# Reordering the first loads, copies and sines of a gated FFT/GEGLU backward kernel

## The chip, the cores and the metric

The kernel runs on one core of a Trainium2 chip. The metric is device time in microseconds (us) for one execution of the whole program. Engines are named as in the profile: PE (TensorE), DVE (VectorE), ACT (ScalarE), POOL (GpSimd) and SP (SyncE, which here only issues DMAs).

## The reference

The program computes a forward result and the gradients for all inputs but B_x. There are two branches over the same x of 2048 rows by 576 columns: a 2-D real FFT, multiplied with a complex weight and transformed back, and a gated GELU feed-forward of inner width 4608. A sigmoid gate per row mixes them.

```
x = A_x
g = sigmoid((x * gate_w).sum(-1, keepdims=True))
a = irfft2(rfft2(x) * (w_r + 1j * w_i))
b = (gelu(x @ w_gate) * (x @ w_up)) @ w_down
out = g * a + (1 - g) * b
outputs: out, and the gradients of x, w_r, w_i, w_gate, w_up, w_down, gate_w for a given grad_out (dO)
```

## The kernel before

**Stages.** The first part runs over 18 groups g of 256 columns of the inner width, and in each over four steps m of four row tiles (128 rows each). A step computes z = dO w_down^T and xy = x [w_gate | w_up], squeezes them through the GELU and its derivative, and stores A, dHu and dHg to DRAM scratch. Matmuls for the gradients of the weights of the group before, and units of the FFT branch, are put between. A last part multiplies the stored tiles with the weights for b and the gradient of x; it takes the last 428 us or so and is pure PE work.

**Order.** The order of the work is written out by hand: each engine runs its instructions in the order of the program text, and the framework only adds the semaphores. A DMA that is issued from SP may first wait for an older DMA whose semaphore it takes over.

**Head.** [...]dO, x and w_down are transposed by PE. `titems` (L367) returns three closures for four row tiles: column chunks 0 and 1, chunks 2 and 3, chunk 4. Each transposes into one PSUM tile (L378, L381, L384) and copies it out (L385) by the engine that is passed: `VC` is a DVE copy, `AC` an ACT copy. The PSUM tiles come from `pgtile` and `phtile`, two buffers each, so a third closure on the same kind of tile waits for the first one's copy. Ahead of the loop stand: 30 dummy matmuls (L896), six small ones that lay gate_w on partitions (L901) and their casts to gwT (L905, L907), sine tables for the columns (`build_D`: y on POOL or DVE at L130 and L131, the angles on DVE at L136 and L138, the sines on ACT at L141 and L142), the transposes of dO tiles 0 to 3 into dOT, and those of the first 256 rows of w_down (wdn) into wdT.

**First step, g = 0 and m = 0.** `H_mm` issues z's matmuls over chunks 0 to 3 (L413), then `opening` (L918), then z's last chunk (L418) and the first part of xy (L422). `opening` transposes x tiles 0 to 3, makes the second and third group of sines, `parity` (L107 to L110), the masked tail tables (`tails`, L148 to L152), the row angles of tiles 0 to 3 (`build_R`, L165 and L172), and the gate of these four tiles (`gate`, L390: 20 matmuls at L394, a sigmoid at L396, two small ACT instructions). Then follow the transposes of dO tiles 4 to 7 (`do1`), the rest of xy (L429), the transposes of x tiles 4 to 7 (`x1`), the evacuation of xy by ACT (`H_act`, L448 to L451), row angles of tiles 4 to 7 (`build_R`, L169 to L172), small column constants (`columns_B`, L187 on), the gate of the next four tiles, the first third of the transposes of dO tiles 8 to 11 (`do2`), and the first half of the elementwise work (`H_ew1`, L456 to L460, DVE). Its second half (`H_ew2`, L476 to L497) runs within the next step, as `held`. The same pattern with fewer transposes holds for m = 1 and m = 2.

Of the kernel before, what the change touches and what calls it, by code (L numbers as in the profile page):

```python
# [9 lines left out]
ACT = mybir.ActivationFunctionType  # L10
ALU = mybir.AluOpType
BF16 = mybir.dt.bfloat16
# [27 lines left out]
LO, HI = slice(0, 64), slice(64, 128)  # L40
# [4 lines left out]
def eo(c):  # L45

    return slice(256 * (c % 2) + c // 2, 256 * (c % 2) + 256, 2)
# [41 lines left out]
def iotas_R(nc, tb, res, unit):  # L89
    G, V = nc.gpsimd, nc.vector  # L90
    kw = dict(allow_small_or_imprecise_dtypes=True)
    tb.qcol_i = res.tile([P, 1], I32, name="qcol_i")
    G.iota(tb.qcol_i[:], pattern=[[0, 1]], base=0, channel_multiplier=1)
    kk = tb.kk = unit([2, P], F32, name="kk")
    tb.krow = kk[:, 0, :].rearrange("p (g k c) -> p g k c", k=2, c=2)
    for v in range(2):
        G.iota(tb.krow[:, :, v, :], pattern=[[1 - 2 * v, 32], [0, 2]], base=64 * v, channel_multiplier=0, **kw)
    G.memset(tb.krow[:, 0, 1, :], 32.0)
    tb.kadd = kk[:, 1, :].rearrange("p (k c) -> p k c", c=2)
    G.iota(tb.kadd, pattern=[[0, 64], [S // 4, 2]], base=S // 4, channel_multiplier=0, **kw)  # L100
    tb.scol = res.tile([P, T], F32, name="scol")
    G.iota(tb.scol[:], pattern=[[1, T]], base=0, channel_multiplier=16, **kw)
    par_i = res.tile([P, 1], I32, name="par_i")
    tb.par = res.tile([P, 2], F32, name="par_f")

    def parity():
        V.tensor_single_scalar(par_i[:], tb.qcol_i[:], 1, op=ALU.bitwise_and)  # L107
        V.tensor_copy(tb.par[:, 1:2], par_i[:])
        V.tensor_scalar(tb.par[:, 0:1], tb.par[:, 1:2], -1.0, 1.0, op0=ALU.mult, op1=ALU.add)
        V.tensor_scalar(tb.kadd[:, 0, 1:2], tb.par[:, 1:2], float(S // 2), float(S // 4), op0=ALU.mult, op1=ALU.add)  # L110
    return parity
# [7 lines left out]
def build_D(nc, tb, unit, c0, n):  # L119

    V = nc.vector
    step = 2.0 * math.pi / D
    TS = (nc.gpsimd if c0 else V).tensor_scalar
    X = unit([n, HF], F32, name="XD")
    y = unit([n, HF], F32, name="yD")
    for c in range(n):
        TS(y[:, c, :], tb.lrow[:], tb.dn[:, c0 + c:c0 + c + 1], MAGIC, op0=ALU.mult, op1=ALU.add)  # L130
    TS(y[:], y[:], -MAGIC, -float(D), op0=ALU.add, op1=ALU.mult)  # L131
    o = unit([n, 2, HF], name="Dt")

    def angles():
        for c in range(n):
            V.scalar_tensor_tensor(X[:, c, :], tb.lrow[:], tb.dcol[:, c0 + c:c0 + c + 1], y[:, c, :],  # L136
                                   op0=ALU.mult, op1=ALU.add)
        V.scalar_tensor_tensor(y[:], X[:], -1.0, X[:], op0=ALU.mult, op1=ALU.max)  # L138

    def sines():  # L140
        nc.scalar.activation(o[:, :, 0, :], y[:], ACT.Sin, bias=tb.halfpi[:], scale=-step)  # L141
        nc.scalar.activation(o[:, :, 1, :], X[:], ACT.Sin, scale=-step * EPS_SCALE)  # L142
        if c0 < 4:
            tb.Dt += [o[:, c] for c in range(n)]

    def tails():
        tl = unit([2, 2, 2, HF], name="Dt")
        nc.gpsimd.memset(tl[HI, 0], 0.0)  # L148
        nc.gpsimd.memset(tl[LO, 1], 0.0)
        for k, r in enumerate((LO, HI)):  # L150
            for par in range(2):
                V.tensor_scalar(tl[r, k, par], o[r, 0], tb.par[r, par:par + 1], None, op0=ALU.mult)  # L152
        tb.Dt += [tl[:, k, par] for k in range(2) for par in range(2)]
    return angles, sines, tails
# [101 lines left out]
def kernel(  # L256
# [4 lines left out]
    nc = tc.nc  # L261
    LD = nc.sync
# [6 lines left out]
    unit = Unit(ctx.enter_context(tc.tile_pool(name="unit", bufs=NUNIT, side="right")), "unit")  # L269
# [27 lines left out]
    wts = {}  # L297
# [26 lines left out]
    def load_x(t0):  # L324
        LD.dma_start(xn[:, t0:t0 + 4, :], x_v[:, t0:t0 + 4, :])

    def load_do(t0):
        LD.dma_start(dB[:, t0:t0 + 4, :], do_v[:, t0:t0 + 4, :])

    ident = res.tile([P, P], BF16, name="ident")  # L330
    make_identity(nc, ident[:])
    gwr = unit([D], name="gwr")
    nc.scalar.dma_start(gwr[0:1, :], gate_w.rearrange("(o d) -> o d", o=1))
    load_do(0)
    wdn = unit([2, D], name="wdn")
    LD.dma_start(wdn[:], B_w_down[0:FG, :].rearrange("(c p) d -> p c d", p=P))
    load_x(0)
    load_w(0, 0, nc.scalar)
    for k in range(1, 4):
# [2 lines left out]
    tb = iotas(nc, res, unit)  # L342
# [27 lines left out]
    def titems(src, dst, t0, ps, copies, n=4):  # L370

        def item(k, cs):
            def f():
                tp_ = ps[k](BF16).rearrange("p (j t m) -> p j t m", j=2, t=4)
                for j, c in enumerate(cs):
                    for tt in range(n):
                        if c < 4:
                            nc.tensor.transpose(tp_[:, j, tt, :], src[:, t0 + tt, eo(c)], ident[:])  # L378
                        elif n < 4:
                            for r in (LO, HI):  # L380
                                nc.tensor.transpose(tp_[r, 0, tt, :], src[:, t0 + tt, 512:D], ident[:])  # L381
                        else:
                            c0 = (t0 + tt) * D + (512, D - P)[tt % 2]
                            nc.tensor.transpose(tp_[:, 0, tt, :], src[:].rearrange("p t d -> p (t d)")[:, c0:c0 + P], ident[:])  # L384
                copies[k](dst[:, cs[0]:cs[0] + len(cs), t0:t0 + n, :], tp_[:, 0:len(cs), 0:n, :])  # L385
            return f
        return [item(k, cs) for k, cs in enumerate(((0, 1), (2, 3), (4,)))]

    def gate(k):
        lps = pgtile()  # L390
# [510 lines left out]
        nc.tensor.matmul(gps[r, c:c + 1], lhsT=w, rhs=one[:], start=True, stop=True)  # L901
    D0 = build_D(nc, tb, unit, 0, 2)
    D0[0]()
    D0[1]()
    AC(gwT[:, 0:4], gps[:, 0:4])  # L905
    for c, r in ((4, LO), (5, HI)):
        AC(gwT[r, c:c + 1], gps[r, c:c + 1])  # L907
    D2 = build_D(nc, tb, unit, 2, 2)
    D2[0]()
    D4 = build_D(nc, tb, unit, 4, 1)  # L910
    parity = iotas_R(nc, tb, res, unit)
    for f in titems(dB, dOT, 0, (pgtile, pgtile, phtile), (VC, AC, VC)):
        f()
    for f in titems(wdn, wts[0][1][:].rearrange("p k (c m) -> p k c m", c=2), 0, (phtile, pgtile, phtile), (AC, VC, VC), n=2):
        f()
    makeB = build_B(nc, tb, unit, res)

    def opening():  # L918
        for f in titems(xn, xT, 0, (pgtile, pgtile, pgtile), (VC, AC, VC)):
            f()  # L920
        D2[1]()
        D4[0]()
        D4[1]()
        parity()
        D4[2]()
        build_R(nc, tb, unit, 0)
        gate(0)

    fg = zipped(*fwd_units(xT, scr_x, None)) + zipped(*fwd_units(dOT, scr_g, gs32))
# [62 lines left out]
    for g in range(NG):  # L992
# [3 lines left out]
        for m in range(NPR):  # L996
# [15 lines left out]
            if g == 0:  # L1012
# [28 lines left out]
                for part in range(2):  # L1041
                    H_act(1, xy, tiles, part)
                if m == 0:
                    build_R(nc, tb, unit, 4)
                    columns_B(nc, tb, res)
                elif m == 1:
                    next(makeB)
# [312 lines left out]
```

## Time and profile before

| | |
|---|---|
| median of 3 runs | 1395.96 us (1395.55 to 1396.18) |
| the profiled execution | 1396.09 us, span 1394.3 us |
| PE clock granted | 1.00 |
| z of m=0, 1, 2, 3 starts at | 8.60, 21.76, 30.73, 39.58 us |
| z of the second group starts at | 45.64 us |

The span is what the engines' instructions cover; the device time has a little more at both ends. A timeline row reads: start in us, duration in us, engine, line, operation, output and inputs, shapes, number of merged instructions, and in brackets how long the engine was idle before and what ended it. Durations of merged rows overlap a little with the row behind them, so the distance from start to start is the better measure of a rate.

Where the DMAs stand in the head:

| load, in order of SP's queue | issued at us | landed at us |
|---|---|---|
| dO tiles 0 to 3, 576 KB | 0.75 | no record; first used at 5.12 |
| wdn, 288 KB | 1.20 | 5.8 |
| x tiles 0 to 3, 576 KB | 1.67 | 7.9 |
| w_gate of group 0, 256 KB | 2.18 | no record |
| w_up of group 0, 256 KB | 4.93 | no record |
| dO and x tiles 4 to 7 | 6.11, 7.79 | no record; first used at 13.88 and 17.81 |
| dO and x tiles 8 to 11 | 8.17, 8.64 | 15.2, 16.5 |
| dO and x tiles 12 to 15 | 9.12, 9.62 | 18.0, 19.6 |

### The profile page before, as it was taken

Reading aid. Unit: us, or ns where it says so; the run is one execution under the profiler, and the core shown is the slowest. Engines: PE = TensorE matmul, PEld = TensorE weight load, DVE = VectorE, ACT = ScalarE, POOL = GpSimd, SP = SyncE. Lnnn points to the kernel's source line nnn. Section 1 sums busy time; section 2 is a strip of 40 time slices with the busy share of each in tenths; the row PEclk is TensorE's granted clock in tenths of the full one; section 3 lists DMA queues with packets and bytes.
Section 4 is the critical chain, followed back from the end, with each engine's and each line's share of the span. In section 5 each row is a group of like instructions: output and inputs, shape, how many; then the busy total and the mean of one; then the engine's idle time right before and its main releaser. Section 6 shows DMA issues by size and latency. Waiting matters only on the chain.

```text
span 1394.3 us, 25930 instructions
## 1 busy us (share of the span) xinstructions
PE 1372.9 (98%) x10186; PEld 914.3 (66%) x10272; DVE 740.2 (53%) x1406; ACT 710.8 (51%) x1311; POOL 245.6 (18%) x486
## 2 busy tenths in 40 slices
PE   8999999999999999999999999999999999999999
PEld 6556566566566556556566566556777777777777
DVE  7975656555889777885656666560001742211101
ACT  7877767777787878767767777661000000000000
POOL 3001011123345634412111101110000100000000
PEclk9999999999999999999999999999999999999999
DMA  6433445355466656555556465749999998777873
GB/s 216 126 86 110 132 108 132 92 146 157 114 165 157 154 143 164 144 142 135 148 141 170 127 164 154 176 110 279 195 193 200 230 192 169 162 156 166 154 153 90
DMA packets 510646, 214.49 MB, mean 154 GB/s; under 512 B 312538, under 2 KB 503708, under 8 KB 510524
## 3 DMA queue, kind: packets, MB, share of 16 engines
q1 hardware_dynamic: 493402, 187.44, 57.9%
q0 software_dynamic: 14912, 24.24, 6.2%
q8 instruction: 80, 1.31, 0.4%
q10 hardware_dynamic: 2210, 1.15, 0.4%
q14 instruction: 42, 0.34, 0.1%
HBM read 41.05 MB, written 93.84 MB: 97 GB/s over the span
## 4 chain that ended last, share of the span: by engine, by line
PE 90%; ACT 2%; issue 1%; DMA 0%; SPq 0%; DVE 0%; ACTq 0%
PE acc L1210 30%; PE wps L559 16%; PE xy L429 15%; PE wps L541 9%; PE z L413 8%; PE wps L573 2%; PE xy L422 2%; PE pf L602 2%; PE z L418 1%; PE pf L619 1%; PE pf L873 1%; PE pf L800 1%; PE pf L711 1%; PE pf L875 1%; ACT ZT L850 0%
## 5 line engine op out<-in xcount | busy, mean ns | idle before, releaser
L1210 PEld LDWEIGHTS <-pin 128*128 128x128 bf16 x3456 | 338.0, 98 | 85.8 <-issue 0.5
L559 PE MATMUL wps<-dH,xn 128*128 128x512 bf16 x1135 | 269.9, 379 | 1.3 <-DVE dwd L510 0.5
L429 PE MATMUL xy<-wgu,xT 128*128 128x512 bf16 x1083 | 258.2, 379 | 8.3 <-issue 7.0
L429 PEld LDWEIGHTS <-xT 128*128 128x128 bf16 x1152 | 106.5, 98 | 133.0 <-issue 24.8
L559 PEld LDWEIGHTS <-xn 128*128 128x128 bf16 x1152 | 111.5, 98 | 118.6 <-issue 1.3
L1227 ACT COPY bo<-acc 128x288 f32<-128x288 f32 x32 | 12.8, 399 | 305.0 <-PE acc L1210 305.0
L541 PE MATMUL wps<-dB,A 128*128 128x288 bf16 x1152 | 154.2, 286 | 0.7 <-DVE dB L990 0.6
L566 POOL DMA_DIRECT2D out_dram<-dw x134 | 73.0, 548 | 430.4 <-ACT dw L510 389.3
L1210 PE MATMUL acc<-wgT,pin 128*128 128x288 bf16 x1152 | 143.8, 286 | 0.0
L1210 PE MATMUL acc<-wuT,pin 128*128 128x288 bf16 x1152 | 143.6, 286 | 0.0
L1210 PE MATMUL acc<-wd_all,pin 128*128 128x288 bf16 x1152 | 142.6, 286 | 0.0
L413 PE MATMUL z<-wdT,dOT 128*128 128x256 bf16 x1152 | 137.5, 272 | 1.0 <-ACT wdT L385 0.5
L541 PEld LDWEIGHTS <-A 128*128 128x128 bf16 x1152 | 112.1, 98 | 34.3 <-issue 1.3
L441 ACT ACTIVATE da<-z,omg 128x256 bf16<-128x256 f32 x288 | 112.3, 473 | 32.9 <-PE z L418 32.8
L413 PEld LDWEIGHTS <-dOT 128*128 128x128 bf16 x1152 | 112.5, 98 | 23.1 <-issue 2.2
L450 ACT CAST xb<-xy 128x512 bf16<-128x512 f32 x144 | 85.3, 593 | 48.0 <-PE xy L429 47.6
L1282 DVE SCALAR_TENSOR_TENSOR f32t<-gwf,dlog,b16t 128x576 f32<-128x576 f32 x16 | 13.1, 817 | 172.2 <-DMA b16t<-dxa_scr 172.2
L448 ACT ACTIVATE q<-xy 128x512 bf16<-128x512 f32 x144 | 87.9, 614 | 7.0 <-PE xy L429 4.7
L451 ACT CAST hu<-xy 128x512 bf16<-128x512 f32 x144 | 87.5, 608 | 0.0
L487 DVE TENSOR_TENSOR xb<-xb,sg 128x1024 bf16<-128x1024 bf16 x48 | 33.1, 691 | 96.6 <-ACT sg L479 96.5
L510 ACT CAST dw<-wps 128x512 bf16<-128x512 f32 x72 | 42.3, 590 | 54.5 <-PE wps L559 52.3
L456 DVE TENSOR_SCALAR s<-q 128x1024 bf16<-128x1024 bf16 x72 | 30.6, 425 | 69.9 <-ACT q L448 69.7
(220 smaller groups left out, 1636.7 us busy)
## 6 DMA issues: line engine op xcount, KB each, us to landing
scr<-dH SPq DMA_DIRECT2D x144, 256.0 KB, 3.4
scr<-A SPq DMA_DIRECT2D x72, 256.0 KB, 2.7
out_dram<-dw POOLq DMA_DIRECT2D x134, 64.0 KB, 2.5
wd_all<-in_B_w_down_dram SPq DMA_DIRECT2D x3, 1728.0 KB, 9.9
out_dram<-dwd POOLq DMA_DIRECT2D x34, 144.0 KB, 2.9
scr_p<-Vt SPq DMA_DIRECT2D x32, 145.0 KB, 2.9
wgu<-in_B_w_gate_dram SPq DMA_DIRECT2D x18, 256.0 KB, 4.1
wgu<-in_B_w_up_dram SPq DMA_DIRECT2D x18, 256.0 KB, 3.4
```

What stands on the lines that cost most here:

```text
L413: nc.tensor.matmul(zo(t), lhsT=dOT[:, ci, t, :], rhs=wdT[:, ci, :], start=(t % 4 < 2 and ci == 0), stop=False)
L429: nc.tensor.matmul(xy[k][:, t % 2, :], lhsT=xT[:, ci, t, :], rhs=wgu[:, ci, :], start=False, stop=(ci == 3))
L441: nc.scalar.activation(da[:, t, :], z[:, t % 2, t // 2, :], ACT.Copy, scale=omg32[:, 4 * m + t:4 * m + t + 1])
L448: nc.scalar.activation(q[:, h, :], xy[:, :, 0:FG], ACT.Square)
L450: nc.scalar.copy(xb[:, h, :], xy[:, :, 0:FG])
L451: nc.scalar.copy(hu[:, h, :], xy[:, :, FG:2 * FG])
L487: V.tensor_tensor(xb[:], xb[:], s[:], op=ALU.mult)
L510: wcopy[0](out, in_)
L541: nc.tensor.matmul(wps[:, :288], lhsT=tl(0, t)[:, fch * P:(fch + 1) * P], rhs=dB[:, t, h * 288:(h + 1) * 288], start=(t == 0), stop=(t == ...
L559: nc.tensor.matmul(wps[:].rearrange("p a b -> p (a b)"), lhsT=xn[:, t, c * P:(c + 1) * P], rhs=kt[t // 4][1][:, t % 4].rearrange("p k f -> ...
L566: wst[0].dma_start(ov[:, c, fsl], dw[:, k, :])
L1210: nc.tensor.matmul(acc[:, :288], lhsT=src[:, r, :], rhs=w_of(r)[:, h * 288:(h + 1) * 288], start=(first and r == 0), stop=(last and r == F ...
```

## The change

Six edits, none of which changes what is computed:

- wdn is loaded ahead of dO, and dO tiles 0 to 3 come in two DMAs of two tiles.
- The casts to gwT go from ACT to DVE.
- wdn is transposed ahead of dO, its copies by DVE, ACT, DVE (before: ACT, DVE, DVE).
- dO tiles 0 to 3 are transposed by pairs of tiles, four chunks into one PSUM tile (`pair`), copied by DVE and ACT; their chunk 4 stays with `titems`. The first sines, `D0[1]`, come behind that.
- In `opening` the sines of D2 and D4 come ahead of the transposes and copies of x, and a one-column sigmoid, whose result nobody uses, behind them. The angles of D4 move ahead of the loop.
- `parity`, the tail tables and the row angles of tiles 0 to 3 move from `opening` to the end of step m = 0, ahead of the row angles of tiles 4 to 7.

```diff
-    def load_do(t0):
-        LD.dma_start(dB[:, t0:t0 + 4, :], do_v[:, t0:t0 + 4, :])
+    def load_do(t0, n=4):
+        LD.dma_start(dB[:, t0:t0 + n, :], do_v[:, t0:t0 + n, :])
...
-    load_do(0)
     wdn = unit([2, D], name="wdn")
     LD.dma_start(wdn[:], B_w_down[0:FG, :].rearrange("(c p) d -> p c d", p=P))
+    load_do(0, 2)
+    load_do(2, 2)
     load_x(0)
...
+    def pair(src, dst, t0, ps, cp):
+
+        tp_ = ps(BF16).rearrange("p (c t m) -> p c t m", c=4, t=2)
+        for c in range(4):
+            for tt in range(2):
+                nc.tensor.transpose(tp_[:, c, tt, :], src[:, t0 + tt, eo(c)], ident[:])
+        cp(dst[:, 0:4, t0:t0 + 2, :], tp_)
...
     D0 = build_D(nc, tb, unit, 0, 2)
     D0[0]()
+    VC(gwT[:, 0:4], gps[:, 0:4])
+    for c, r in ((4, LO), (5, HI)):
+        VC(gwT[r, c:c + 1], gps[r, c:c + 1])
+    for f in titems(wdn, wts[0][1][:].rearrange("p k (c m) -> p k c m", c=2), 0, (phtile, pgtile, phtile), (VC, AC, VC), n=2):
+        f()
+    pair(dB, dOT, 0, pgtile, VC)
+    pair(dB, dOT, 2, pgtile, AC)
+    titems(dB, dOT, 0, (None, None, phtile), (None, None, VC))[2]()
     D0[1]()
-    AC(gwT[:, 0:4], gps[:, 0:4])
-    for c, r in ((4, LO), (5, HI)):
-        AC(gwT[r, c:c + 1], gps[r, c:c + 1])
     D2 = build_D(nc, tb, unit, 2, 2)
     D2[0]()
     D4 = build_D(nc, tb, unit, 4, 1)
+    D4[0]()
     parity = iotas_R(nc, tb, res, unit)
-    for f in titems(dB, dOT, 0, (pgtile, pgtile, phtile), (VC, AC, VC)):
-        f()
-    for f in titems(wdn, wts[0][1][:].rearrange("p k (c m) -> p k c m", c=2), 0, (phtile, pgtile, phtile), (AC, VC, VC), n=2):
-        f()
...
     def opening():
+        D2[1]()
+        D4[1]()
+        nc.scalar.activation(tb.warm[:], tb.halfpi[:], ACT.Sigmoid)
         for f in titems(xn, xT, 0, (pgtile, pgtile, pgtile), (VC, AC, VC)):
             f()
-        D2[1]()
-        D4[0]()
-        D4[1]()
-        parity()
-        D4[2]()
-        build_R(nc, tb, unit, 0)
         gate(0)
...
                 if m == 0:
+                    parity()
+                    D4[2]()
+                    build_R(nc, tb, unit, 0)
                     build_R(nc, tb, unit, 4)
                     columns_B(nc, tb, res)
```

## The prediction

> **What bounds the kernel now.** I read the shares of busy time first. TensorE (PE) fills the span, so a change at the head pays only if it moves the time at which PE works on, and keeps it moved until the stages behind it.
>
> ```profile
> PE 1372.9 (98%) x10186; PEld 914.3 (66%) x10272; DVE 740.2 (53%) x1406; ACT 710.8 (51%) x1311; POOL 245.6 (18%) x486
> ```
>
> Next the timeline of the head, engine by engine. ScalarE (ACT) first: after its copy of x it runs four sines and loads a table before the sigmoid of the gate.
>
> ```profile
> 8.60 1.91 PE L413 MATMUL z<-wdT,dOT 128*128 128x256 bf16 x16 [0.52 <-ACT wdT L385]
> 11.44 1.01 ACT L385 COPY xT<-pf 128x1024 bf16<-128x1024 bf16 x1 [2.89 <-PE pf L378]
> 12.35 0.54 ACT L141 ACTIVATE Dt<-yD,halfpi 128x290 bf16<-128x290 f32 x1
> 12.50 0.69 PE L394 MATMUL pf<-gwT,xT 128*128 128x1 bf16 x20 [0.38 <-ACT xT L385]
> 13.95 1.28 ACT L396 ACT_TABLE_LOAD   x1
> 15.47 0.61 PE L378 MATMUL pf<-ident,dB 128*128 128x128 bf16 x8 [0.97 <-ACT g_bf L396]
> ```
>
> The bracket is the idle time before the instruction and what ended it: z waits for the last wdT copy, the gate for ACT's copy of x, and the second transpose of the next dO for the sigmoid. Then VectorE (DVE), from the end of step m=0:
>
> ```profile
> 19.82 1.02 DVE L385 COPY xT<-pf 128x1024 bf16<-128x1024 bf16 x2 [0.62 <-PE pf L378]
> 20.76 0.22 DVE L169 TENSOR_SCALAR k<-kk 128x128 int32<-128x128 f32 x1
> 23.28 0.42 DVE L456 TENSOR_SCALAR s<-q 128x1024 bf16<-128x1024 bf16 x1
> 25.34 0.42 DVE L385 COPY dOT<-pf 128x512 bf16<-128x512 bf16 x1
> 28.03 1.02 DVE L385 COPY xT<-pf 128x1024 bf16<-128x1024 bf16 x2 [2.27 <-PE pf L378]
> 36.21 0.42 DVE L385 COPY dOT<-pf 128x512 bf16<-128x512 bf16 x1
> 36.68 0.61 PE L378 MATMUL pf<-ident,xn 128*128 128x128 bf16 x8 [0.17 <-DVE dOT L385]
> 67.70 3.08 PE L541 MATMUL wps<-dB,A 128*128 128x288 bf16 x20 [0.61 <-DVE dB L990]
> ```
>
> Last, busy time by stretch (PE, PEld, DVE, ACT, POOL, clock, DMA share, GB/s):
>
> ```profile
> 8.60:13.10 4.50, 3.78 (x56) 3.35 (x55) 1.60 (x4) 1.66 (x3) 0.00 (x0) 1.00 1.01 355
> 28.00:44.00 16.00, 15.62 (x163) 10.27 (x163) 14.72 (x27) 14.32 (x31) 1.61 (x6) 1.00 0.28 83
> 44.00:60.00 16.00, 15.33 (x96) 8.28 (x95) 14.87 (x27) 11.95 (x22) 0.00 (x0) 1.00 0.33 100
> ```
>
> The reader is to see two regimes. Up to about 20 us DVE has room (1.60 of 4.50 us). From 28.0 to 68 us it works almost without a break (14.7 and 14.9 of 16 us), and PE stands behind it at 36.68 (dOT copy) and at 67.70 (scaled dB). The ACT wait on L457 at 44.68, behind which PE waits for hu at 48.70, belongs to the same chain. **So what counts is not when z starts but when DVE gets to its 28.03 copies.**
>
> **What the Trainium skill says.** "ScalarE: Activation LUTs", section "What ACT_TABLE_LOAD costs", gives 1283 ns for the load and about 1380 ns of drain. The trace agrees on the load (1.28 us) and shows no drain: L396 starts at 15.24, 1.29 us after the load. I take 1.28. "TensorE: Matmul & The Clock Gate", section "What's actually happening", has PE at half clock until some 3.4 us of activity, and again after an idle window of that length. The trace agrees for the start: 16 weight loads of dB take 1.62 us from 5.12, 100 ns each, while 8 of wdn from 7.04 take 0.49, some 60 each; nothing here shows a return to the low clock, since no wait of the head is longer than 1.4 us. The same page ("Architectural detail") calls ACT and DVE strict first-in first-out; the timelines agree, and it is why each moved instruction delays all that is queued behind it.
>
> **Part 1: loads.** wdn (288 KB) goes ahead of dO, and dO's 576 KB come in two halves. The bytes up to the end of dO are the same, and wdn now lands last at 5.83, so the second half lands there, the first half with wdn at about 4.9 (dO, 576 KB, is there at 5.12 today). One more DMA is one more SP issue (0.42 us) ahead of xn, the weights and the later tiles. SP's issues also wait for older transfers (u at 4.93 waits 2.0 us for dB), so g, u and dB(1) may leave up to 2 us later. Bounds: 0 to +0.7 us of arrival. xn landed at 7.9 and is used at 10.24, later tiles have more room: I take nothing.
>
> **Part 2: first copies.** gwT's three casts go from ACT (6.14 to 6.50) to DVE, where they fit between the first angles (end 4.85) and the first wdT copy: nothing. D2's angles (4.77 to 5.90) go behind the dO copies, D4's (0.71) behind those. PE: 12 transposes of wdn from 5.12 at 100 ns end at 6.3, pair 0 is through at 7.0, pair 1 at about 7.5, the last chunk at 7.7. Copies start 0.38 us after the eighth weight load, as at 6.20 today: pair 0 on DVE 7.40 to 8.09, chunk 4 to 8.46; pair 1 on ACT 7.8 to 8.8. z starts on pair 0 at 8.12 and its second half at 8.97 finds pair 1 ready: **z starts 0.48 us earlier**, and so do the transposes of x (9.76).
>
> **Part 3: ACT ahead of x.** Behind pair 1 ACT now has, in start-to-start times of today's rows: copy 0.91, D0 0.76 (5.38 to 6.14), D2 0.77, D4 0.65 (13.30 to 13.95), table 1.28, small sigmoid 0.11. D2's angles are done by 9.5, D4's by 10.2, in time. 7.8 + 4.48 = 12.3: only then the copy of x, which PE would have had ready at 10.96. It ends at 13.36, and **the gate starts at 13.42 instead of 12.50, 0.92 later**. In return the sigmoid follows at once. From gate to L429 PE needs 0.62 (gate), 0.12, 0.64, 0.47 and 0.39 = 2.24 us (rows 12.50 to 14.35 without the wait, then 15.47 to 15.86), where it took 3.36. L429 starts at 15.66 instead of 15.86: a gain g of 0.2 us. DVE's copies at 19.82 move by the same.
>
> **Part 4: masks and row angles.** Parity, four masks and the first row angles leave 13.12 to 16.52 on DVE (3.40 less 0.26 of waiting = 3.1 us), which costs PE nothing there. They go between 20.76's row angles and the copies before, on a DVE with 2.55 us of small work and H_ew1 ahead. The two POOL memsets (0.58, 0.57) move with them; POOL is idle from 7.8 to 23.5: nothing. The dOT copy of 25.34 moves by 3.1 - 0.2 = 2.9 and ends at 28.68. The x transposes of m=1 need its PSUM buffer, as 36.68 shows for m=2. They start at 27.17 now, start at 28.73 then: **+1.56 us**; the 2.27 us idle before 28.03 absorbs the rest. Behind this DVE is full up to 68 us and PE follows it, so the whole delay is kept; after that PE sets the pace, and nothing in the page is tied to absolute time.
>
> **Sum.** +1.56 against the own span of 1394.3, whose run took 1396.09, beside a median of 1395.96 over runs 0.63 apart: 1395.96 + 1.5 = **1397.5 us**. In general: shift = 1.76 - g, and g = 13.62 - (start of the gate).
>
> **Rivals.** (A, 58 in 100) as above, own range 1396.3 to 1398.7, from g of -0.7 to 1.2. (B, 22) The pause of PE ahead of the gate, from about 11.4 to 13.4 with 0.5 before it, brings the low clock back. For: the page's idle window. Against: matmuls lie in most windows of 3.4 us. Up to 3.4 us of work at half speed cost 1.7, so g = -1.5 and the shift 3.3: 1399.2. (C, 20, not slower) The ACT queue isn't in the way: pair 1 is copied early, the sines overlap z, and x is copied when PE has it, gate at about 11.9. Place: ACT between pair 1 and x; price: 1.5 us of the 4.48; it decides from a gate start of 11.86, where 1.76 - g is zero. For: ACT idles 2.89 us there today. Against: seven rows with measured durations. With z at 7.5 the gate starts at 11.4: -0.45, so 1395.5. That wdn lands no sooner for being issued first would be a rival on Part 2 alone: z at 8.6, ACT at 8.3, half a microsecond worse, inside A.
>
> **Chances and range.** About 0.2%, 2.8 us, is what a measurement of this kernel can tell from no change. A lies within it but for its upper tail (8 of 58, for delays that later stages add); B lies above; C is within it, except that another order of loads and buffers may shorten waits later (PE idles 21 us in all): 7 of its 20. Faster 0.07, same 0.63, slower 0.30. Range for 8 in 10: from 1394.4 (most of C) to 1400.2 (B with 1 us of drift).
>
> **What would show it.** z near 8.1; gate near 13.4 behind an ACT copy at 12.3 that follows a table load; no wait for g_bf; DVE without its 2.27 us pause before the x copies of m=1, and PE waiting there 1.5 us for dOT; the 67.70 matmul at about 69.2. A gate before 11.9, or DVE idle again in m=1, would prove the forecast wrong.

## The result, and the profile after

| | before | after |
|---|---|---|
| median of 6 runs each | 1395.78 us (1395.53 to 1396.18) | 1400.36 us (1397.79 to 1401.99) |
| ratio, 95% interval | | 1.0032 [1.0019, 1.0044] |
| profiled execution, span | 1394.3 us | 1399.6 us |
| granted PE clock in it | 1.000 | 0.997 |

The change makes the kernel 4.6 us slower, and wide: before, six runs lie within 0.65 us, after within 4.2. The forecast was 1397.5 us with a range up to 1400.2; the median lies just above the range. The first sign of the reason is in the table: the clock isn't full. Of the six executions after, the two at a clock of 1.000 took 1397.79 and 1399.03 us, the four below it 1400.20 to 1401.99.

The timeline of PE in the profiled execution after (start, duration, what ran, and in brackets the idle time before it with what ended it). L403 is the gate (L394 before), L438 the rest of xy (L429), L385 the last chunk of the x transposes (L384), L550 the first gradient of the weights (L541).

```profile
7.46 0.62 PE L395 MATMUL pf<-ident,dB 128*128 128x128 bf16 x8 [0.29 <-DMA dB<-in_grad_out_dram]
8.14 2.09 PE L422 MATMUL z<-wdT,dOT 128*128 128x256 bf16 x16
13.79 0.64 PE L403 MATMUL pf<-gwT,xT 128*128 128x1 bf16 x18 [1.24 <-ACT xT L386]
17.43 0.63 PE L438 MATMUL xy<-wgu,xT 128*128 128x512 bf16 x1
18.28 2.48 PE L438 MATMUL xy<-wgu,xT 128*128 128x512 bf16 x6 [0.22 <-issue]
32.40 0.38 PE L385 MATMUL pf<-ident,xn 128*128 128x128 bf16 x4 [1.24 <-DVE dOT L386]
41.59 0.61 PE L379 MATMUL pf<-ident,xn 128*128 128x128 bf16 x8 [0.51 <-DVE dOT L386]
72.61 3.08 PE L550 MATMUL wps<-dB,A 128*128 128x288 bf16 x20 [0.61 <-DVE dB L998]
```

z starts at 8.14, as forecast (8.12). The gate starts at 13.79 (forecast 13.42, before 12.50). Then comes what the forecast gave a chance of 22 in 100: six matmuls of L438 take 2.48 us from 18.28, some 410 ns each, where the kernel before ran seven in 1.89 (270 each, with their overlap):

```profile
15.91 1.89 PE L429 MATMUL xy<-wgu,xT 128*128 128x512 bf16 x7
```

The z of m=1, at 24.72, is 2.96 us late; z of m=2 (35.29) is 4.56 late, z of m=3 (44.49) 4.91, L550 at 72.61 4.91, and the first matmul of the last part, at 971.48, 4.86. So all but 0.4 us of what is lost is lost by 45 us and then kept; the 0.4 are lost behind the last matmul (see e9 and e10).

ACT's timeline after shows why the gate is late:

```profile
8.12 1.01 ACT L396 COPY dOT<-pf 128x1024 bf16<-128x1024 bf16 x1 [1.33 <-PE pf L395]
9.03 0.54 ACT L141 ACTIVATE Dt<-yD,halfpi 128x290 bf16<-128x290 f32 x1
11.33 1.28 ACT L932 ACT_TABLE_LOAD   x1
12.73 0.99 ACT L386 COPY xT<-pf 128x1024 bf16<-128x1024 bf16 x1
14.46 0.17 ACT L405 ACTIVATE g_bf<-pf 128x4 bf16<-128x4 f32 x1 [0.73 <-PE pf L403]
```

From the dO copy to the copy of x lie 4.61 us without a gap (forecast 4.48), and the dO copy itself comes 0.32 us after its forecast 7.8, since PE had to wait for the second half of dO (0.29 us at 7.46). The sigmoid then follows without a table load, as meant.

Two stretches of the profile after (stretch, its length, busy time of PE, PEld, DVE, ACT and POOL with their instructions, granted PE clock, DMA share, GB/s):

```profile
10.30:13.70 3.40, 1.39 (x21) 1.06 (x18) 1.26 (x3) 3.37 (x7) 0.00 (x0) 0.97 1.02 407
13.75:20.20 6.45, 6.20 (x48) 3.73 (x50) 1.38 (x2) 2.14 (x7) 0.00 (x0) 0.50 1.02 342
```

While ACT works through its queue, PE is busy for 1.39 of 3.40 us. Right behind that the clock is 0.50 for 6.8 us, with PE then busy 6.20 of 6.45. In the kernel before, the emptiest stretch of that length holds 2.05 us of PE work, and the clock in its profile stays at 1.00:

```profile
12.10:15.50 3.40, 2.05 (x38) 1.44 (x37) 2.95 (x13) 3.25 (x8) 0.00 (x0) 1.00 1.02 384
```

DVE's timeline after, end of step m=0:

```profile
29.43 0.43 DVE L465 TENSOR_SCALAR s<-q 128x1024 bf16<-128x1024 bf16 x1
30.38 0.69 DVE L466 TENSOR_TENSOR s<-xb,s 128x1024 bf16<-128x1024 bf16 x1 [0.53 <-DVE s L465]
31.93 0.42 DVE L386 COPY dOT<-pf 128x512 bf16<-128x512 bf16 x1
32.26 1.01 DVE L386 COPY xT<-pf 128x1024 bf16<-128x1024 bf16 x2
35.84 1.12 DVE L501 TENSOR_SCALAR xb<-s 128x1024 bf16<-128x1024 bf16 x1
```

The 2.27 us that DVE idled before its x copies of m=1 are gone (31.93 to 32.26, no bracket): the moved masks fill them, and PE waits 1.24 us for the dOT copy at 32.40. Two things there were in no forecast: L466 starts 0.95 us after L465, with 0.53 idle, and L501 takes 1.12 us. In the kernel before, the counterpart of L466 comes 0.52 us behind that of L465 (which starts at 23.28), and that of L501 takes 0.43:

```profile
23.80 0.69 DVE L457 TENSOR_TENSOR s<-xb,s 128x1024 bf16<-128x1024 bf16 x1
31.62 0.43 DVE L492 TENSOR_SCALAR xb<-s 128x1024 bf16<-128x1024 bf16 x1
```

### The profile page after: what moved, and what is told of

It reads as the page before. It is cut to its first block, busy times and chain, and to the rows that moved or that the text cites. A ratio compares the mean times of both kernels' runs of the same rounds, so it can differ in the third digit from the quotient of the medians.

```text
span 1399.6 us, 25934 instructions
## 1 busy us (share of the span) xinstructions
PE 1375.9 (98%) x10186; PEld 915.0 (65%) x10272; DVE 741.5 (53%) x1409; ACT 710.8 (51%) x1309; POOL 247.5 (18%) x486
## 3 DMA queue, kind: packets, MB, share of 16 engines
q8 instruction: 80, 1.31, 0.4%
q10 hardware_dynamic: 2210, 1.15, 0.3%
## 4 chain that ended last, share of the span: by engine, by line
PE 92%; ACT 3%; DVE 3%; issue 1%; DMA 1%; SPq 0%; DVEq 0%; ACTq 0%
PE acc L1221 30%; PE wps L568 16%; PE xy L438 16%; PE wps L550 10%; PE z L422 8%; PE wps L582 2%; PE xy L431 2%; PE pf L611 2%; PE z L427 2%; PE pf L628 1%; PE pf L882 1%; PE pf L809 1%; PE pf L720 1%; PE pf L884 1%; PE pf L856 0%
## 5 line engine op out<-in xcount | busy, mean ns | idle before, releaser
L438 PE MATMUL xy<-wgu,xT 128*128 128x512 bf16 x1083 | 259.5, 380 | 8.5 <-issue 7.2
L438 PEld LDWEIGHTS <-xT 128*128 128x128 bf16 x1152 | 107.0, 98 | 133.9 <-issue 26.5
L550 PE MATMUL wps<-dB,A 128*128 128x288 bf16 x1152 | 154.2, 286 | 0.7 <-DVE dB L998 0.6
L550 PEld LDWEIGHTS <-A 128*128 128x128 bf16 x1152 | 112.1, 98 | 34.3 <-issue 1.4
L465 DVE TENSOR_SCALAR s<-q 128x1024 bf16<-128x1024 bf16 x72 | 30.6, 425 | 69.9 <-ACT q L457 69.5
```

The lines of the kernel that those rows point to most:

```text
L438: nc.tensor.matmul(xy[k][:, t % 2, :], lhsT=xT[:, ci, t, :], rhs=wgu[:, ci, :], start=False, stop=(ci == 3))
L550: nc.tensor.matmul(wps[:, :288], lhsT=tl(0, t)[:, fch * P:(fch + 1) * P], rhs=dB[:, t, h * 288:(h + 1) * 288], start=(t == 0), stop=(t == ...
```

## The experiments

Each kernel is the changed one ("after") or the one before, with the edit shown. "Gate", "L438", "z" are starts less those of the kernel before (12.50; 15.91 with L438's counterpart L429; 21.76, 30.73, 39.58 for z of m=1, 2, 3; 966.62 for the first matmul of the last part), each from one profiled execution (where the gate's row is split, its longer part counts); the span is against 1394.3. In the expectations theory 1 is the account by a late gate, masks on DVE and the half clock; the other theories and rivals are explained there.

| kernel | median us | before, same chip | ratio [95%] | gate | L438 | z m=1 | z m=2 | z m=3 | last part | span |
|---|---|---|---|---|---|---|---|---|---|---|
| after (profile above) | 1400.36 | 1395.78 | 1.0032 [1.0019, 1.0044] | +1.29 | +1.52 | +2.96 | +4.56 | +4.91 | +4.86 | +5.3 |
| e0, after again | 1399.53 | 1396.01 | 1.0021 [1.0014, 1.0028] | -0.09 | -1.00 | +0.37 | +1.97 | +2.31 | +2.24 | +4.2 |
| e1, filler | 1398.44 | 1395.87 | 1.0020 [1.0013, 1.0027] | +1.24 | +0.03 | +0.02 | +1.63 | +1.98 | +1.93 | +3.5 |
| e2, masks back | 1397.66 | 1395.87 | 1.0011 [1.0005, 1.0018] | +0.68 | -0.54 | -0.54 | -0.54 | -0.54 | -0.62 | -0.2 |
| e3, masks only | 1396.54 | 1395.87 | 1.0006 [0.9998, 1.0015] | +0.08 | +0.08 | +0.08 | +1.24 | +0.92 | +0.86 | +0.9 |
| e4, sines back | 1397.73 | 1395.87 | 1.0013 [1.0007, 1.0020] | -0.53 | -0.72 | -0.72 | +0.86 | +1.21 | +1.15 | +1.6 |
| e5, columns first | 1399.40 | 1396.01 | 1.0025 [1.0016, 1.0033] | +0.61 | -0.29 | -0.29 | +1.93 | +1.60 | +1.53 | +2.0 |
| e6, sines only | 1394.97 | 1396.01 | 0.9991 [0.9985, 0.9998] | -0.25 | -1.37 | -1.10 | -1.10 | -1.11 | -1.14 | -1.1 |
| e7, combined | 1394.78 | 1396.01 | 0.9991 [0.9985, 0.9998] | -0.86 | -1.99 | -1.71 | -1.71 | -1.71 | -1.80 | -1.4 |
| e8, POOL later | 1398.46 | 1396.07 | 1.0016 [1.0006, 1.0025] | +0.46 | -0.76 | -0.76 | +0.84 | +1.19 | +1.14 | +3.5 |
| e9, loads only | 1397.85 | 1396.07 | 1.0013 [1.0007, 1.0020] | +0.70 | +0.96 | +2.37 | +2.37 | +2.37 | +2.37 | +2.8 |
| e10, combined, old loads | 1396.13 | 1396.07 | 0.9997 [0.9989, 1.0005] | -0.42 | -1.54 | -1.27 | -1.27 | -1.27 | -1.32 | -1.3 |
| e11, POOL held | 1398.46 | 1396.10 | 1.0014 [1.0007, 1.0020] | +0.33 | -0.89 | -0.89 | +0.10 | -0.23 | -0.05 | +0.4 |

The row of e1 shows how to read it: the gate is 1.24 late, the wait for the sigmoid that is gone makes that good by L438, the masks cost 1.96 between z of m=1 and of m=3, and it is kept until the last part. From there to the span of 3.5 another 1.6 us are lost, of which more below.

### e0: the change once more

No edit.

> The changed kernel as it is, beside the others on this chip. Theory 1 (moved DVE work costs 1.9 us at the start of group 1, PE's clock halved for one or two windows costs 1.5 us each): executions with a mean clock of 1.000 at about 1397.8 us, those at 0.999 at about 1399.3, at 0.997 to 0.998 at 1400.5 to 1402; median near 1400. Rival: the spread is that of the loads, and goes across the clocks.

19 executions, 1397.53 to 1402.24 us. Sorted by their granted clock they fall apart: eight at 1.000 have the median 1397.66 (1397.53 to 1398.04), seven at 0.999 have 1399.93, four at 0.997 or 0.998 have 1401.4. At full clock the kernel takes the forecast's 1397.5 within 0.2 us; the groups below full clock, 11 of 19 executions, lie 2.3 and 3.7 us higher. (The median of all 19, 1399.53, is inside the forecast's range, 2.0 above its middle.) In the profiled execution of e0 (clock 0.999) the clock is at half from 14.27 us for 3.41 us (columns as above),

```profile
14.27:17.68 3.41, 3.19 (x15) 1.67 (x14) 1.38 (x2) 1.02 (x3) 0.00 (x0) 0.50 1.01 409
```

and in the one above from 13.5 us for 6.83, twice as long. So there can be one stretch of 3.4 us at half clock, or two.

### e1: filler matmuls in PE's pause

```diff
+        fill = phtile()
+        for _ in range(30):
+            nc.tensor.matmul(fill[:, :P], lhsT=ident[:], rhs=ident[:], start=True, stop=True)
         gate(0)
```

> The changed kernel plus 30 dummy matmuls of the identity between the transposes of x tiles 0 to 3 and the gate (they fill PE's pause of about 2 us there; nothing else moves). Theory 1 (two costs: DVE work moved into a stretch where DVE is full, shift 1.76 - g; and, in most executions, PE's clock halved from about 13.5 us because of the pause): the clock stays 1.00, g = 13.62 - 13.8 = -0.2, so +1.9 us, about 1397.7 us, and all executions within 0.7 us of each other. Theory 2 (all of the loss is the moved DVE work; the halved clock is hidden behind DVE): 1400.4 us as for the change. Theory 3 (the loads in their new order are late, PE waits for data): 1400.4 us.

PE's timeline with the filler:

```profile
11.64 1.84 PE L937 MATMUL fx<-ident 128*128 128x128 bf16 x30
13.74 0.60 PE L403 MATMUL pf<-gwT,xT 128*128 128x1 bf16 x18 [0.23 <-ACT xT L386]
15.94 1.89 PE L438 MATMUL xy<-wgu,xT 128*128 128x512 bf16 x7
29.47 0.38 PE L385 MATMUL pf<-ident,xn 128*128 128x128 bf16 x4 [1.25 <-DVE dOT L386]
```

The gate is as late as in the kernel after (13.74), but L438 runs at full speed and starts at 15.94 rather than 17.43, and 20 of 21 executions have a clock of 1.000. **That the pause of PE brings the low clock back is thereby shown**: work of no use in the pause takes it away, with loads, ACT's queue and masks unchanged. The shift of z of m=3 is then 1.98, as expected. The time is not: the median is 1398.44 instead of 1397.7, and the executions lie 3.4 us apart instead of 0.7, nearly all at full clock. So in the medians the filler takes away 1.1 us (e0 1399.53) of the 2.0 by which e0 passes the forecast. The profiled execution (1399.88) lost 1.14 us in the last part and 0.43 behind it (under "what stays open").

### e2, e3: the masks put back, and the masks alone

```diff
 e2, on after
     def opening():
...
+        parity()
+        D4[2]()
+        build_R(nc, tb, unit, 0)
         gate(0)
...
                 if m == 0:
-                    parity()
-                    D4[2]()
-                    build_R(nc, tb, unit, 0)
```

e3 is the opposite edit, on the kernel before: these three lines go from `opening` to the end of m = 0.

> The changed kernel with parity, tail tables and first row angles put back into the first step, between the copies of x and the gate, where DVE idles for 4.5 us in the changed kernel. Theory 1: the DVE part of the loss goes, the pause of PE stays: executions at full clock at +0.2 us (1396.0), those with the halved clock at +3.0 (1398.8), a median between with a wide spread. Theory 2: 1395.8 us, no loss left, narrow. Theory 3: 1400 us.

> The kernel before with only the masks, parity and first row angles moved to the end of the first step. Theory 1: g = 0, so +1.8 us by the formula of the prediction: 1397.5 us, clock 1.00, PE waiting about 1.6 us for the dO copy in m = 1. Theory 2: +4.6 us, 1400.4. Theory 3: no loss, 1395.8.

With the masks back, nothing is lost behind L438: -0.54 stays -0.54. Six executions at full clock have the median 1396.16, fourteen at 0.999 have 1397.91: one stretch of half clock costs 1.75 us here.

The masks alone cost the kernel before 0.86 us in the profile, half of what was expected. The medians differ by 0.7, which their interval (0.9998 to 1.0015) doesn't separate from no change. In PE's timeline of e3 the wait is at the last chunk of the x transposes, not the first:

```profile
29.08 0.38 PE L384 MATMUL pf<-ident,xn 128*128 128x128 bf16 x4 [0.81 <-DVE dOT L385]
```

So it is this group that needs the PSUM buffer of the dOT copy in m=1. It is due 0.61 us after the first group (29.08 - 0.81 - 27.66), so that much less of the masks' time shows than forecast. In e1 the same wait is 1.25, and the masks cost 1.96 in all. Where the other 1.1 come from is left to e5, e8 and e11.

### e4: the sines put back

```diff
     def opening():
-        D2[1]()
-        D4[1]()
-        nc.scalar.activation(tb.warm[:], tb.halfpi[:], ACT.Sigmoid)
         for f in titems(xn, xT, 0, (pgtile, pgtile, pgtile), (VC, AC, VC)):
             f()
+        D2[1]()
+        D4[1]()
         gate(0)
```

> The changed kernel with the sines of D2 and D4 behind the copies of x again, and without the unused sigmoid. Theory 1: ACT copies x when PE has it, the gate starts near 12.3, the sigmoid waits for sines and table load and comes near 15.0, the next dO transposes 0.3 us earlier than in the kernel before: g = 0.3, +1.5 us, 1397.3 us, clock 1.00 throughout. Theory 2: 1400.4 us. Theory 3: 1400 us.

The gate is early (11.97), but the sigmoid stands behind sines and table again, and PE waits for it:

```profile
14.75 0.61 PE L379 MATMUL pf<-ident,dB 128*128 128x128 bf16 x8 [0.77 <-ACT g_bf L405]
```

20 of 21 executions are at full clock: in the profiled one the emptiest 3.4 us hold 2.13 us of PE work. What is left is the masks: -0.72 becomes +1.21 between m=1 and m=3.

### e6: only the sines, in the kernel before

```diff
+    D4[0]()
     makeB = build_B(nc, tb, unit, res)
     def opening():
+        D2[1]()
+        D4[1]()
+        nc.scalar.activation(tb.warm[:], tb.halfpi[:], ACT.Sigmoid)
         for f in titems(xn, xT, 0, (pgtile, pgtile, pgtile), (VC, AC, VC)):
             f()
-        D2[1]()
-        D4[0]()
-        D4[1]()
```

> The kernel before, with only the D2 and D4 sines and the unused sigmoid ahead of the copies of x (D4's angles behind the wdT copies). ACT is free from 8.55 us there: 0.8 + 0.65 + 1.28 + 0.11 end at 11.4, when x is ready (11.44). Theory 1: the gate stays at 12.5, the sigmoid comes at 13.3 instead of 15.2, PE gains 0.8 to 1.1 us and keeps it: 1395.0 us, clock 1.00. Rival (sines ahead of x always cost): the gate is late by 0.9 us, 1396.8.

ACT's timeline of e6:

```profile
9.60 1.28 ACT L922 ACT_TABLE_LOAD   x1
11.19 1.01 ACT L385 COPY xT<-pf 128x1024 bf16<-128x1024 bf16 x1
12.98 0.17 ACT L396 ACTIVATE g_bf<-pf 128x4 bf16<-128x4 f32 x1 [0.78 <-PE pf L394]
```

In this order ACT is done with D0's sines before its dO copy (6.80) is due, and is free from 8.2; the sines of D2 and D4, the table and the small sigmoid (8.19 to 11.10) then end about when x is ready (its copy starts at 11.19, against 11.44). All 21 executions are at full clock, and the kernel is 1.04 us faster (0.92 beside the executions of the kernel before at full clock). **The move of the sines is good in itself. It is D0's sines and the later dO copy, which the changed kernel puts ahead of them, that make ACT late.**

### e7, e10: a combination, and the old order of loads in it

e7 is after with D0's and D2's sines ahead of the dO copies, D4's angles ahead of chunk 4's copy, and the masks in the opening:

```diff
     D0[0]()
+    D0[1]()
+    D2 = build_D(nc, tb, unit, 2, 2)
+    D2[0]()
+    D4 = build_D(nc, tb, unit, 4, 1)
     VC(gwT[:, 0:4], gps[:, 0:4])
...
+    D2[1]()
     pair(dB, dOT, 0, pgtile, VC)
     pair(dB, dOT, 2, pgtile, AC)
+    D4[0]()
     titems(dB, dOT, 0, (None, None, phtile), (None, None, VC))[2]()
-    D0[1]()
...
     def opening():
-        D2[1]()
...
+        parity()
+        D4[2]()
+        build_R(nc, tb, unit, 0)
         gate(0)
...
```

e10 is e7 with dO in one DMA ahead of wdn, as before.

> The changed kernel, rearranged: D0's and D2's sines in ACT's free time between 5 and 8 us, D4's angles ahead of the copy of chunk 4, masks and first row angles back in the first step. Theory 1: ACT is free for x at about 11.1, the gate starts at 12.3, L438 at 14.5 instead of 15.86, a gain of 1.0 to 1.3 us kept to the end, clock 1.00: 1394.7 us; late second halves of dO take up to 0.6 of it. Rival: the pair loads lose more than the sines gain, 1396 or more.

> The combined kernel (sines of D0 and D2 ahead of the dO copies, masks in the opening, dO by pairs) with the loads in the order of the kernel before, so that wdn comes behind dO while PE transposes wdn first. If wdn is there by 5.8 us and the new load order brings only a late second half of dO: gate at 12.0, z at 8.1, shift -1.3 and no loss behind the last matmul: 1394.7, no different from the combined kernel's 1394.8. If wdn first is worth its half microsecond: 1395.3.

PE's timeline of e7:

```profile
11.64 0.69 PE L403 MATMUL pf<-gwT,xT 128*128 128x1 bf16 x20 [0.38 <-ACT xT L386]
13.92 1.89 PE L438 MATMUL xy<-wgu,xT 128*128 128x512 bf16 x7
```

e7 is the fastest kernel of the study: 1394.78 us, 1.2 under the kernel before and 4.75 under e0 on the same chip, all 21 executions at full clock. e10 missed its expectation. Its profiled execution is as expected (head 1.3 us early, span 1393.0 beside e7's 1392.9), but that is the fastest of 13, which run from 1394.75 to 1396.96 with a median of 1396.13: no gain over the kernel before, where 1394.7 was expected. In the profiled one PE waits 0.80 us for wdn before it can start at 5.97, since wdn comes behind dO; whether that wait varies was not seen. The loads that cost the kernel before 1.8 us (e9) thus go with the faster of the two combined kernels, though e7 and e10 ran on different chips.

What e9 and e10 settle is the end of the program. From the start of PE's last merged row to the end of the span the kernel before takes 1394.3 - 1386.71 = 7.59 us, e9 1397.1 - 1389.08 = 8.02, e10 1393.0 - 1385.39 = 7.61, and after and e7 8.03 and 7.99. Measured from the end of PE's last matmul it is 3.03 us in the four kernels with the old loads (before, e3, e6, e10) and 3.45 or 3.46 in all ten with the new ones. So the new loads (another order, and one DMA more) cost 0.4 us behind the last matmul, and nothing else of the change does. Which of the two does it, and by what means, isn't seen in the traces.

### e9: only the loads, in the kernel before

```diff
-    load_do(0)
     wdn = unit([2, D], name="wdn")
     LD.dma_start(wdn[:], B_w_down[0:FG, :].rearrange("(c p) d -> p c d", p=P))
+    load_do(0, 2)
+    load_do(2, 2)
```

> The kernel before with the changed order of loads alone (wdn first, dO in two halves). If the loads cost what the changed kernel's trace shows, the transposes of dO tiles 2 and 3 wait for the second half, landing at 6.8 to 7.4 us instead of 5.1, PE reaches z 1.0 to 1.5 us late, and the shift that is kept is 1.0 to 1.5: 1397.2. If the loads cost nothing, as Part 1 of the prediction has it (second half at 5.8): z 0.5 us late at most, 1396.3. The 0.4 us that the kernels with the new loads lose behind the last matmul should appear here in either case if the loads are its cause.

PE's timeline, and the stretches around the low clock (columns as above):

```profile
5.89 1.67 PE L379 MATMUL pf<-ident,dB 128*128 128x128 bf16 x14 [0.37 <-DMA dB<-in_grad_out_dram]
16.87 3.31 PE L430 MATMUL xy<-wgu,xT 128*128 128x512 bf16 x8
```

```profile
12.80:16.20 3.40, 2.05 (x38) 1.44 (x37) 2.95 (x13) 3.26 (x8) 0.00 (x0) 1.00 1.03 405
16.20:19.60 3.40, 3.40 (x15) 1.73 (x15) 2.27 (x6) 1.92 (x6) 0.00 (x0) 0.52 1.08 364
```

The loads alone cost 1.8 us in the median, and 1.6 of it also at full clock (twelve executions, 1397.57, against thirty of the kernel before, 1395.95). The profiled one accounts for 1.1 of the 1.6, the late gate and the end of the program; the rest wasn't seen. In it PE waits 0.37 us for dO, the gate is 0.70 late, and behind a stretch with 2.05 us of PE work the clock goes to half: eight matmuls of L430 take 3.31 us. Nine of 21 executions have a clock under 1.000. The kernel before has a stretch of the same 2.05 us, keeps its clock in its profile, and shows one under 1.000 in 10 of 62, 6 of 65, 8 of 38 and 6 of 23 executions, in four sets. So at 2.05 of 3.4 us the clock is lost in some executions and kept in most.

### e5, e8, e11: what the masks do besides queueing

```diff
 e5, on e1
                 if m == 0:
+                    columns_B(nc, tb, res)
                     parity()
                     D4[2]()
                     build_R(nc, tb, unit, 0)
                     build_R(nc, tb, unit, 4)
-                    columns_B(nc, tb, res)
```

> The changed kernel with the 30 dummy matmuls of e1, and columns_B ahead of the masks at the end of step 0 instead of behind them, so that POOL's small instructions run beside other DVE work. In e1 the moved masks cost 1.96 us, in e3 only 0.84, and DVE lost 0.53 us ahead of L466 and 0.69 in L501 in e1, not in e3. Theory P (DVE and POOL exclude each other at that moment): L501 back at 0.43 us, the shift at the start of group 1 falls from 1.98 to between 0.9 and 1.5. Theory S (it lies in the tiles that these instructions touch): both losses stay, shift 2.0, 1398.4 us as in e1.

L501 was 0.43 us, as theory P says, but L465 took 0.88 with 0.52 idle behind it, now beside two POOL memsets and an iota that had come to run there. The clash was moved, not taken away, and the shift of 1.60 lies between what both theories expected. Inconclusive on P and S. But e5 bears on the clock: 7 of its 12 executions had 0.999, in spite of the filler. In its profile PE waits 1.86 us for the dOT copy (to 29.76), in a stretch that holds only 1.51 us of PE work:

```profile
26.35:29.75 3.40, 1.51 (x13) 0.78 (x11) 2.88 (x6) 2.32 (x3) 3.02 (x7) 1.00 0.21 60
```

The clock is kept in this execution; where the seven lost it was not profiled.

```diff
 e8, on e1: columns_B returns its POOL half as a closure, called at m == 3
                     build_R(nc, tb, unit, 4)
-                    columns_B(nc, tb, res)
-                elif m == 1:
+                    colrest = columns_B(nc, tb, res)
+                elif m == 3:
+                    colrest()
                     next(makeB)

 e11, on e8: the cast on DVE that POOL needs goes into the closure too
-    V.tensor_copy(col[:, 0:4], bit[:])
     def rest_():
+        V.tensor_copy(col[:, 0:4], bit[:])
```

> This is the filler kernel with one thing more: the POOL half of columns_B (15 one-column operations) and the iotas behind it run at the end of step m=3 instead of m=0 and m=1. DVE's own instructions keep their places. Theory P (POOL and DVE keep each other out): L465 and L466 of step m=0 lose their gap of 0.53 us and L501 goes from 1.12 to about 0.43 us; the shift of z of m=2 against the kernel before falls from 1.63 us to about 0.6, and of m=3 from 1.98 to about 0.9; the time falls by some 0.7 to 1.1 us under the filler kernel, to about 1397.4. Theory S (the delay is DVE's own queue alone): z of m=2 and m=3 stay 1.6 and 2.0 us late, 1398.4.

> The filler kernel again, with the POOL half of columns_B held back for real: the cast of L189 on DVE, which the first POOL operation needs, moves with it to the end of step m=3 (in e8 POOL still started at 26 us, because nothing stood in its queue). DVE loses 0.1 us of work in step m=0, all else of it keeps its place. Theory P (POOL and DVE keep each other out): in step m=0 the pair L465 and L466 starts 0.52 us apart instead of 0.95, L501 takes 0.43 instead of 1.12 us, and the x transposes of m=1 follow the gate 1.1 us sooner: z of m=2 starts 0.5 to 0.6 us late where the gate is 1.24 us late, and by as much less where the loads come earlier, against 1.63 and 0.84 in the filler kernel and e8. Theory S (DVE's own queue alone): L501 stays at 1.12 us, and z of m=2 follows the gate as in those two. In either case executions go on spreading by 3 us, since the last part isn't touched.

e8 doesn't delay POOL: POOL has nothing else in its queue, so it started its half at 25.97, as soon as DVE's cast was done, whatever the place in the text. It still gives a close pair with e11, in which POOL starts at 51.06 and DVE has 0.1 us less to do in step m=0. DVE's and POOL's timelines of e8:

```profile
25.71 0.43 DVE L468 TENSOR_SCALAR s<-q 128x1024 bf16<-128x1024 bf16 x1
26.66 0.69 DVE L469 TENSOR_TENSOR s<-xb,s 128x1024 bf16<-128x1024 bf16 x1 [0.53 <-DVE s L468]
32.12 1.12 DVE L504 TENSOR_SCALAR xb<-s 128x1024 bf16<-128x1024 bf16 x1
26.31 0.34 POOL L198 TENSOR_TENSOR bcol<-bcol 128x1 f32<-128x1 f32 x2
32.08 0.87 POOL L226 IOTA k2B<- 128x128 f32 x1
```

and of e11:

```profile
25.39 0.43 DVE L468 TENSOR_SCALAR s<-q 128x1024 bf16<-128x1024 bf16 x1
25.92 0.69 DVE L469 TENSOR_TENSOR s<-xb,s 128x1024 bf16<-128x1024 bf16 x1
31.37 0.43 DVE L504 TENSOR_SCALAR xb<-s 128x1024 bf16<-128x1024 bf16 x1
51.06 0.51 POOL L195 TENSOR_SCALAR bcol<-bcol 128x1 f32<-128x1 f32 x2 [43.28 <-DVE g L1069]
```

With POOL out of the way the gap of 0.53 us is gone and L504 takes 0.43 instead of 1.12. In e8, L469 starts at 26.66, when POOL's operation ends (26.31 + 0.34). From z of m=1 to z of m=3 e8 loses 1.19 + 0.76 = 1.95 us, e11 0.89 - 0.23 = 0.66. **So of the masks' price of 1.95 in the head, 1.29 us are POOL and DVE keeping each other out, and 0.66 DVE's own queue.** Two reservations: at z of m=2 e11 is +0.10, where its expectation, scaled to its gate, asks for about -0.35, and by the last part e11 has lost 0.18 of the gain again. e3, where POOL's operations fell beside other ones and L501's counterpart took 0.43, agrees with 0.84. "SBUF — State Buffer" of the Trainium skill, section "Who interferes with whom", says that a DVE instruction with two SBUF inputs contends with a GpSimd (POOL) instruction that reads SBUF, that one in a two-port mode contends with GpSimd too, and that whoever issues first has the shared ports for its whole instruction. The runs agree for the first: 0.53 us of waiting of a two-input operation behind a POOL operation that reads SBUF. The 0.69 us of L504 beside the iota fit the second, if L504 runs in such a mode, which no trace shows.

What this is worth in the time isn't shown: the medians of e1, e8 and e11 are all near 1398.4 although their profiled heads differ by 2.2 us; only the fastest executions (1397.48, 1397.57 and 1396.47) show some of it. See below.

## Why the prediction failed

**At full clock the number of A came out, in part by luck.** Eight executions of e0 at a clock of 1.000 have the median 1397.66, against 1397.5. The chain of A holds in e1: gate at 13.74, g by the formula 13.62 - 13.74 = -0.12, shift 1.76 + 0.12 = 1.88, measured 1.98. But 1397.5 leaves out the 0.4 us behind the last matmul, the gate comes anywhere from 12.41 (e0) to 13.79 in the same kernel, the masks' price is right from wrong terms (Part 4), and e1, with 20 of 21 executions at full clock, has the median 1398.44. "The whole delay is kept" holds from z of m=3 to the last part, within 0.2 us in every kernel of the table, but three executions then lose more (below).

**The step that failed is the one that keeps PE at full clock: rival B was given 22 in 100.** The prediction saw the pause of PE ahead of the gate, named the half clock, and set it aside with "matmuls lie in most windows of 3.4 us". It asked whether a matmul lies in the stretch, and should have summed PE's busy time in it, by its own numbers: x's last transposes end at about 11.4, the gate comes at 13.4, so in the 3.4 us up to there PE has at most 1.4 us of work, against 2.05 in the emptiest stretch of the kernel before. "TensorE: Matmul & The Clock Gate" of the Trainium skill, section "What's actually happening", which the prediction leant on, puts the low clock behind an idle window; here a stretch that was 40% busy was enough. The table puts the emptiest 3.4 us of each profiled execution (from 5.5 us to PE's last matmul) beside the share of executions whose clock is under 1.000:

| kernel | PE busy in its emptiest 3.4 us | clock under 1.000 |
|---|---|---|
| after, e0 | 1.31, 1.38 | 4 of 6, 11 of 19 |
| e2 | 1.31 | 15 of 21 |
| e5 | 1.50, behind the filler, at 26.4 us | 7 of 12 |
| before | 2.05 | 10 of 62, 6 of 65, 8 of 38, 6 of 23 |
| e9, e3 | 2.05 | 9 of 21, 1 of 13 |
| e1, e8, e4 | 2.11, 2.12, 2.13 | 1 of 21, 0 of 10, 1 of 21 |
| e11 | 2.57 | 1 of 20 |
| e6, e7, e10 | 2.67, 2.67, 2.68 | 0 of 21, 0 of 21, 1 of 13 |

Together that is 37 of 58 executions up to 1.50 us, 40 of 222 at 2.05, and 4 of 127 from 2.11 on. Each stretch is taken from one execution, and a kernel's stretch can differ in others. The filler of e1 shows that the pause is the cause; the table alone would not.

The price that the prediction gave B, "up to 3.4 us at half speed cost 1.7", was right for one stretch: in e9 the gate is 0.70 late and z of m=1 2.37, which is 1.67 more. In e0 the gate is 0.09 early; at full clock e1 gains 1.22 from there to z of m=1, e0 comes out 0.37 late instead, so 1.68 are lost. What was not considered is a second stretch: by the same sum after loses 2.96 - 1.29 + 1.22 = 2.89. (The 2.27 between e0's groups is more, since other things differ between executions: its profiled one lost 1.53 in the last part.) The shift of the profiled execution is composed as follows: gate 1.29; half clock 2.89 less 1.22, mostly the sigmoid's wait that is gone; masks 4.91 - 2.96 = 1.95; end of the program 0.4; sum 5.3, the difference of the spans.

**Part 1, "I take nothing", failed too.** The second half of dO was to land at 5.83. PE waited for it at 7.46 (after), 7.42 (e1) and 5.89 (e9); in e0, e8 and e11 no wait for it shows, and z starts at 7.0 to 7.4. (Part of z's spread is PE's own: four transposes of wdn take 0.40 us in e0 and 0.61 in after, which still runs at the low clock of its start.) e9 shows the price in the kernel before: a gate 0.70 late, the clock lost in 9 of 21 executions, 0.4 us at the end. The bound of 0.7 was put on the later loads, where no loss was seen.

**Part 2** gives z at 8.12, and 8.14 is seen in after; but in e0, the same kernel, z starts at 7.01, so that the close hit is luck. **Part 3** holds in its mechanism; the gate is 0.37 later than forecast, 0.32 of it from the late dO. **Part 4** has the right sum from the wrong terms. The masks were to cost 1.76 through the PSUM buffer of the first x transposes of m=1. It is the last of them that waits (e3), and DVE's queue costs 0.66 to 0.84; the other 1.29 is the clash of POOL with DVE. The prediction asked of POOL only whether it has time ("POOL is idle from 7.8 to 23.5"), not what its column operations do to DVE's when both have moved. Two errors nearly cancelled.

**Rival C** didn't happen, but e6 shows that its condition, an ACT that is free before x is ready, is what makes the move of the sines pay.

**What stays open.** (1) At full clock executions of one kernel still lie apart by 3.1 to 4.2 us in e1, e5, e8, e9 and e11, by 2.3 or less in the other kernels, and by 0.5 in the eight of e0. The changed loads or the moved masks alone don't sort them: e9 has its masks in the old place, and e0 has both changes. A part is seen in the profiled executions. The span of each is accounted for within 0.02 us by its shift at the first matmul of the last part, the 0.42 us of the new loads, and what the last part itself loses: 1.53 in e0, 1.14 in e1, 1.90 in e8, nothing in any other. In these three PE waits for the tiles that it reads from the scratch (in e8 also for ACT); first e8, then e1 and e0:

```profile
PE acc L1228 <- DMA pin<-scr: 1.1, 1, 1.1
PE acc L1228 <- ACT bo L1245: 0.5, 1, 0.5
PE acc L1224 <- DMA pin<-scr: 1.0, 1, 1.0
PE acc L1221 <- DMA pin<-scr: 0.9, 2, 0.5
```

So the delay at the head is not all: DMAs of the last part can be late too; why they are in some executions isn't shown. (2) Why dO's second half lands up to 1.6 us later in one execution than in another. (3) Whether all work of PE counts alike for its clock: in the stretch of after (10.30 to 13.70) it is transposes of x, but for two matmuls of the gate, and the filler consists of ordinary matmuls.

## What to carry to other kernels

An order on a queue is good or bad by when the queue is free: the same sines ahead of the copy of x gain 1 us behind an idle ACT and lose 1 behind one that still has a dO copy and other sines to do. Before PE is made to wait in a place where it waited little, sum its busy time over 3.4 us: in this kernel the clock was lost in most executions where 1.5 us or less of it were work, at a price of 1.7 us for one stretch and 2.9 for two, and hardly ever from 2.1 us on. Useless matmuls can be cheaper than the pause. Work that is moved to another place of DVE is to be held against what POOL does there, and a delay of the head that runs into a full engine was kept here up to the last part.

## What the runs showed of the hardware

- PE's clock went to half for one or two stretches of 3.41 us (6.83 in all) behind 3.4 us in which PE was busy for 1.4 us, with no single wait longer than 1.24 us (after, e0). With 1.3 to 1.5 us of work in the emptiest stretch of the profiled execution 37 of 58 executions had a clock under full, with 2.05 us 40 of 222, and from 2.11 us on 4 of 127.
- A 128x1024 bf16 DVE operation with one input took 1.12 us instead of 0.43 beside a POOL iota of 0.87, and one with two inputs started 0.53 us late behind a POOL operation of 0.34; no wait for POOL is named in the bracket, which puts it on DVE's own instruction before.
- The changed loads at the head (wdn first, dO in two DMAs instead of one) lengthened the end of the program, behind its last matmul, by 0.4 us in all ten kernels that have them.
- The table load of the sigmoid took 1.28 us in before, after and e6, and behind a full queue of ACT the next activation started 1.30 us after the load (11.33 to 12.63 in after).
